# Block-diagonal copies on GpSimd, transposes of 104 partitions, loads of 48 rows and new offsets in the list

## The chip, the cores and the metric

The kernel runs on one core of one Trainium2 chip. The metric is the device time of one execution in microseconds (us). TensorE is called PE in the profile (its weight loads PEld), VectorE DVE, ScalarE ACT, GpSimd POOL, and SyncE, which issues part of the DMAs, SP.

## The reference

Two parts, one after the other. The first is a recurrence with a 40 x 40 state for each of 4 batches and 8 heads over 768 steps:

```python
for t in range(S):
    y[:, :, t] = np.einsum('bhd,bhde->bhe', rt, state)
    Sa = np.einsum('bhde,bhe->bhd', state, at)
    state_decay = state * wt[:, :, None, :] - np.einsum('bhd,bhe->bhde', Sa, bt)
    state = state_decay + np.einsum('bhd,bhe->bhde', vt, kt)
```

The second is an MLP on the 3072 tokens of width 320 that come out of it: `h = x @ w_in` with 2048 columns, `g = h * tanh(softplus(h))`, and `g @ w_out` back to 320. All is float32.

## The kernel before

**Tiling.** The 768 steps are cut into 12 chunks of 64. The 32 heads (batch and head together) are split by two bits, be and al, and by 8 places s. Of a tile's 128 partitions, al chooses the lower or the upper 64, and 40 of each 64 hold the head's 40 dimensions: partitions 0 to 39 and 64 to 103 are used, the rest is zero or filler. The first 104 partitions so hold all that is used.

**Preparation of a chunk, `pre_a(c, be)`** (24 calls). SP loads w and a (tile wa, L322) and b and k (tile bk, L325), each in two DMAs of 40 rows, one for al=0 and one for al=1. VectorE forms running products of w by two scans (L343, L348), scales a in place (L346) and b, k (L354). ScalarE copies a into the block-diagonal tile ad (L352), two copies of 64 partitions. TensorE multiplies ad by bk in groups of 3, 3 and 2 places (L386); the results go to GP and HA (L389 to L397). TensorE then transposes bk by a matmul with the identity in cst, four at a time into one PSUM bank (L410), and ScalarE copies the 40 used columns of each 64 to bkn (L412). GpSimd's queue writes P out to pD (L357).

**Inversion, `inv(n)`** (6 calls, one for each two chunks). VectorE transposes GP into X (L420), runs 30 steps of two small instructions each (L425, L428) that invert all 32 x 32 triangles of the two chunks at once, and transposes the result to TT (L430) and T1 (L432). TensorE forms the lower-left blocks of the 64 x 64 inverses (L444, L452) with a copy by ScalarE between them (L454). For each chunk and be ScalarE then fills the block-diagonal tile bdT: the two diagonal blocks from TT for each al (L466, L467) and the off-diagonal one from PSUM (L468). TensorE multiplies it with HA (L476), ScalarE evicts to KT (L479).

**Steps, `step(c)`** (12 calls). For each half g of the places: `step_a` copies the state ST into VS (L504), multiplies with KT (L514) and evicts u to UVT (L517); `step_b` multiplies UVT by r's block-diagonal tile bdr (L557) and masks into UVQ (L560); `step_u` transposes UVT (L528, L530); `step_d` transposes the state (L544) and evicts it to smd (L546); `step_c` multiplies UVQ by bkn (L586) and smd by bdr (L591), adds the state (L596, L602) and copies y out (L598). The state passes from chunk to chunk, so the steps of a chunk wait for those of the one before. `step_loads` fills VS, UVT and bdr for the next chunk by GpSimd's queue (L487, L491, L494); each of these tiles has one buffer, so the load waits for the last reader of the chunk before.

**MLP.** `convert` loads w_in and w_out and splits them into a high and a low part on ScalarE and VectorE (tile cv, L731 to L739). `load_x` reads y and P back and multiplies them (L792 to L797). `mlp1` (L814) and `mlp2` (L835 to L837) run 6 x 8 times.

**The order.** The program is written as a list of operations, each with the engine, a booked duration, what it reads and writes and, for a DMA, its latency (`lat`) and service time (`srv`). `Plan.order` simulates the engines with these booked numbers and at each point takes, among the ready operations of the engine that is free first, the one with the highest priority: the length of the work that hangs behind it plus an offset from PRIO, by the operation's kind and its chunk (kinds such as 'ld' the loads of a chunk, 'pv' its VectorE part, 'ik' bdT and KT, 'wi' the conversion of w_in). Operations that become ready within LOOK plus an entry of LOOKS of the earliest may be chosen as well. The order that comes out is fixed: each engine and each DMA queue then runs its instructions strictly in it.

The planner books ScalarE's copy to ad like this:

```python
        for al in range(2):
            q = slice(al * 64, al * 64 + 64)
            op('A', 0.62, lambda q=q, al=al: A.copy(ad[q, :, :, al], a[q].rearrange("p (s k t) -> p s k t", k=2, t=32)),
               r=[('a', be, al)], w=[('ad', be, al)])
```

## Time and profile before

| | |
|---|---|
| time, median of 3 runs | 746.27 us (744.09 to 746.48) |
| the profiled execution | 745.79 us, of it 744.0 us span |
| mean granted TensorE clock | 0.965 |
| instructions | 17243 |
| busy, share of the span | PE 91%, PEld 84%, DVE 61%, ACT 57%, POOL 14% |
| DMA | 58206 packets, 61.81 MB |

The span runs from the first to the last instruction of the profiled execution. "Busy" is the time in which an engine worked on at least one instruction; a matmul's end is modelled, and matmuls overlap, so the mean duration of a matmul is longer than the pace at which they follow each other. A line such as "L410 PE MATMUL ps<-cst,bk 128*128 128x128 f32 x192 | 25.4, 282 | 2.4" gives the line in the kernel, the engine and operation, what is written from what (moving operand, then stationary), the shapes (stationary 128*128, moving 128x128), the count, busy us, mean ns of one, and the idle time ahead of them with what ended it. A piece of the chain of waits has its start, its length and what it was. A wait row gives the engine and line that waited, for whom, us in total, how often, and the longest.

### The profile page before, as it was taken

How to read it: one execution, taken by the hardware profiler on the slowest of the kernel's cores; microseconds unless marked ns; L12 is line 12 of the kernel's file. 1: busy time of each engine (PE TensorE's matmuls, PEld its weight loads, DVE VectorE, ACT ScalarE, POOL GpSimd, SP SyncE). 2: the span in 40 equal slices, each digit the busy share in tenths (PEclk: the TensorE clock that was granted, in tenths of full speed). 3: DMA queues.
4: the chain of work that ended last, by engine and by line, in shares of the span. 5: the costliest groups of instructions: out<-in, count | busy, mean ns of one | idle time of the engine just before them, and what ended most of it. 6: DMA issues, size and time to landing. Idle time of an engine off the chain costs nothing.

```text
span 744.0 us, 17243 instructions
## 1 busy us (share of the span) xinstructions
...
## 2 busy tenths in 40 slices
...
GB/s 191 171 98 89 64 39 104 77 139 116 107 109 111 101 118 150 37 117 128 123 220 185 206 46 100 0 12 97 14 1 103 18 1 40 19 0 1 36 1 35
DMA packets 58206, 61.81 MB, mean 83 GB/s; under 512 B 25536, under 2 KB 48704, under 8 KB 58128
## 3 DMA queue, kind: packets, MB, share of 16 engines
...
## 4 chain that ended last, share of the span: by engine, by line
PE 64%; DVE 22%; ACT 7%; issue 4%; DMA 1%; POOL 0%; ACTq 0%; DVEq 0%
PE ps L814 24%; PE ps L835 7%; PE ps L837 7%; PE ps L836 7%; PE ps L557 4%; DVE XL L428 3%; DVE tmp L425 3%; PE ps L386 3%; PE ps L586 3%; DVE P L343 2%; DVE bk L354 2%; PE ps L476 2%; PE ps L528 2%; DVE HA L394 2%; PE ps L591 1%
## 5 line engine op out<-in xcount | busy, mean ns | idle before, releaser
L819 DVE TENSOR_TENSOR gl<-g,gh 128x1024 fp32r<-128x1024 f32 x48 | 58.8, 1225 | 194.9 <-ACT gh L818 188.7
L817 ACT ACTIVATE g<-ps 128x512 f32<-128x512 f32 x96 | 57.0, 597 | 173.6 <-PE ps L814 173.3
L837 PE MATMUL ps<-w_oh,gl 128*128 128x320 f32 x384 | 118.6, 309 | 0.0
L835 PE MATMUL ps<-w_oh,gh 128*128 128x320 f32 x384 | 118.5, 309 | 0.0
L836 PE MATMUL ps<-w_ol,gh 128*128 128x320 f32 x384 | 118.5, 309 | 0.0
L814 PE MATMUL ps<-xh,w_ih 128*128 128x512 f32 x288 | 113.2, 393 | 0.0
L814 PE MATMUL ps<-xh,w_il 128*128 128x512 f32 x288 | 97.7, 393 | 0.0
L386 PE MATMUL ps<-bk,ad 128*128 128x168 f32 x384 | 68.7, 340 | 26.9 <-DVE bk L354 18.2
L386 PEld LDWEIGHTS ps<-bk,ad 128*128 128x128 f32 x384 | 63.8, 215 | 28.8 <-issue 26.5
L814 PE MATMUL ps<-xl,w_ih 128*128 128x512 f32 x192 | 75.4, 393 | 0.0
L836 PEld LDWEIGHTS ps<-w_ol,gh 128*128 128x128 f32 x384 | 72.1, 188 | 2.1
L835 PEld LDWEIGHTS ps<-w_oh,gh 128*128 128x128 f32 x384 | 72.1, 188 | 2.0
L837 PEld LDWEIGHTS ps<-w_oh,gl 128*128 128x128 f32 x384 | 72.1, 188 | 0.0
L814 PEld LDWEIGHTS ps<-xh,w_il 128*128 128x128 f32 x288 | 54.1, 188 | 12.3
L814 PEld LDWEIGHTS ps<-xh,w_ih 128*128 128x128 f32 x288 | 54.2, 188 | 10.6 <-issue 0.2
L428 DVE TENSOR_TENSOR XL<-XL,tmp 128x30 f32<-128x30 f32 (+9 forms) x180 | 58.7, 326 | 2.0
L425 DVE TENSOR_TENSOR tmp<-XL 128x30 f32<-128x30 f32 (+9 forms) x180 | 58.5, 325 | 1.7
L557 PE MATMUL ps<-bdr,UVT 128*128 128x128 f32 x384 | 48.8, 283 | 4.9 <-ACT UVT L517 2.7
L818 ACT CAST gh<-g 128x1024 fp32r<-128x1024 f32 x48 | 50.4, 1050 | 1.5
L557 PEld LDWEIGHTS ps<-bdr,UVT 128*128 128x128 f32 x384 | 46.1, 197 | 6.0 <-ACT UVT L517 3.4
L476 PE MATMUL ps<-bdT,HA 128*104 128x128 f32 x384 | 46.9, 280 | 2.4 <-ACT bdT L468 2.4
L476 PEld LDWEIGHTS ps<-bdT,HA 128*104 128x104 f32 x384 | 44.1, 174 | 4.1 <-ACT bdT L468 2.2
...
## 6 DMA issues: line engine op xcount, KB each, us to landing
...
```

The costliest lines, as they stand in the source:

```text
L386: PE.matmul(pv()[:, j], ad[:, s0 + j].rearrange("p k a t -> p (k a t)"), bk[:, s0 + j], start=(j == 0), stop=True, skip_group_check=True)
L425: op('V', (0.16 + m * i * 0.00104), lambda tv=tv, i=i, m=m: V.tensor_tensor(out=tv, in0=X[:, i + 1:32, i:i + 1].broadcast_to([128, m, i]), ...
L428: op('V', (0.16 + m * i * 0.00104), lambda tv=tv, i=i: V.tensor_tensor(out=X[:, i + 1:32, 0:i], in0=X[:, i + 1:32, 0:i], in1=tv, op=ALU.ad ...
L476: PE.matmul(kv()[:, j], ha.t[:, s0 + j], bd[:, o + s0 + j].rearrange("p a t -> p (a t)"), start=(j == 0), stop=True, skip_group_check=True)
L557: PE.matmul(qv()[:, s], UVT[:, g * 4 + s, be * 128:be * 128 + 128], bdr[:, be, g * 4 + s].rearrange("p a t -> p (a t)"), start=(s == 0), s ...
L814: PE.matmul(b.t, w, x, start=(n == 0), stop=(n == 7), skip_group_check=True)
L817: op('A', 0.6, lambda b=b, j=j: A.activation(g.t[:, j], b.t, AF.Mish), r=[b], w=[(g, j)])
L818: op('A', 1.05, lambda: A.copy(gh.t, g.t), r=[(g, 0), (g, 1)], w=[gh])
L819: op('V', 1.226, lambda: V.tensor_tensor(out=gl.t, in0=g.t, in1=gh.t.bitcast(F32), op=ALU.subtract), r=[(g, 0), (g, 1), gh], w=[gl])
L835: PE.matmul(o, gh.t[:, j, t], oh, start=(f == 0 and j == 0), stop=False, skip_group_check=True)
L836: PE.matmul(o, gh.t[:, j, t], ol, start=False, stop=False, skip_group_check=True)
L837: PE.matmul(o, gl.t[:, j, t], oh, start=False, stop=(f == 7 and j == 1), skip_group_check=True)
```

## The change

- The copies of a into ad (L352) and of the diagonal blocks from TT into bdT (L466, L467) go from ScalarE to GpSimd, booked at 0.6 and 0.35 us.
- The transposes of bk, UVT and the state (L410, L528, L544) read partitions 0 to 103 and use a 104 x 104 identity; four results of 104 columns lie side by side in the bank, and the evictions pick the two times 40 used columns out of each (`heads`). smd keeps 320 elements and 24 of filler, set to zero once, in place of 512.
- The host arrays for w and a, b and k, r and v are padded from 40 to 48 rows per half, and the DMAs move 48 rows. Their booked service times fall.
- PRIO has new numbers in all its rows, and LOOKS, empty before, has entries.

The diff, with the two lists cut to a few rows:

```diff
 LOOK = 0.05
-LOOKS = {}
+LOOKS = {
+    'zero': (0.05, 0.05, 0.15, 0.05, 0.1, 0.1, 0.05,),
+    'ld': (1, 0.05, 0.05, 0,),
...
+}
 PRIO = {
...
-    'wi': (-64.5, -663.5, 78, 201.5, 248.5, 158.5, 616, 742, 588, 148, 305, 685.5,),
...
+    'wi': (-1016, -754.5, -442, -504.5, -596.5, -768, -478, -268.5, -156, -212.5, -71.5, -34.5,),
...
 }
...
     r, k, vv, w, a, b = (v(inp[n]) for n in 'rkvwab')
     o = {}
     wt = w.transpose(4, 2, 1, 6, 3, 0, 5).reshape(nch, 2, 2, 40, 8, C)
-    wa = np.zeros(wt.shape[:4] + (1040,), np.float32)
-    wa[..., :520].reshape(wt.shape[:4] + (8, 65))[..., 1:] = wt
-    wa[..., 528:] = a.transpose(4, 2, 1, 6, 3, 0, 5).reshape(nch, 2, 2, 40, 512)
+    wa = np.zeros((nch, 2, 2, 48, 1040), np.float32)
+    wa[..., 40:, :520].reshape(nch, 2, 2, 8, 8, 65)[..., 1:] = 1
+    wa[..., :40, :520].reshape(nch, 2, 2, 40, 8, 65)[..., 1:] = wt
+    wa[..., :40, 528:] = a.transpose(4, 2, 1, 6, 3, 0, 5).reshape(nch, 2, 2, 40, 512)
     o['wa'] = wa
     bt, kt = (x.transpose(4, 2, 1, 6, 3, 0, 5).reshape(nch, 2, 2, 40, 8, 1, C) for x in (b, k))
     bk = np.concatenate([bt, kt], -2)
     bk[:, 1] = np.concatenate([kt, bt], -2)[:, 1]
-    o['bk'] = bk.reshape(nch, 2, 2, 40, 8, 128)
-    o['rD'] = np.ascontiguousarray(r.transpose(4, 1, 6, 2, 3, 0, 5)).reshape(nch, 2, 40, 16, C)
-    o['vD'] = np.ascontiguousarray(vv.transpose(4, 1, 6, 3, 0, 2, 5)).reshape(nch, 2, 40, 8, 128)
+    pad = lambda x, ax: np.concatenate([x, np.zeros(x.shape[:ax] + (8,) + x.shape[ax + 1:], np.float32)], ax)
+    o['bk'] = pad(bk.reshape(nch, 2, 2, 40, 8, 128), 3)
+    o['rD'] = pad(r.transpose(4, 1, 6, 2, 3, 0, 5).reshape(nch, 2, 40, 16, C), 2)
+    o['vD'] = pad(vv.transpose(4, 1, 6, 3, 0, 2, 5).reshape(nch, 2, 40, 8, 128), 2)
     o['vN'] = np.ascontiguousarray(vv.transpose(4, 2, 5, 3, 0, 1, 6)).reshape(nch, 2, C, 16, 40)
     p = np.arange(128)
     cst = np.zeros((128, 328), np.float32)
...
 
     cst = cs.tile([128, 328], F32, name="cst")
     ident = cst[:, 0:128]
+    used = slice(0, 104)
+    rows = cst[used, 0:104]
+    heads = lambda x: bass.AP(x.tensor, x.offset, [x.ap[0], [104, 4], [64, 2], [1, 40]])
     maskQ = cst[:, 128:192]
     maskH = cst[:, 192:256]
     maskG = cst[:, 296:328]
...
     newRW = make(wk, 4, [128, 2, 16], "rw")
     newR = make(wk, 2, [128, 2, 4], "R")
     newSTN = make(wk, 2, [128, 8, 40], "stn")
-    newSMD = make(wk, 2, [128, 4, 128], "smd")
+    newSMD = make(wk, 2, [128, 344], "smd")
     newYEV = make(wk, 1, [128, 2, 8, 64], "yev")
     newHA = make(ci, NHA, [128, 8, 104], "HA")
     newGP = make(ci, 2, [128, 32, 2, 32], "GP")
...
         op('G', 0.7, lambda t=VS[be]: G.memset(t, 0.0), w=[(k, be, g) for k in ('VSv', 'VSs') for g in range(2)])
         op('G', 0.5, lambda t=ST[be]: G.memset(t, 0.0), w=[('ST', be)])
     op('G', 0.8, lambda: [G.memset(t[:, 640:664], 0.0) for t in S.bkn], w=['bkn0'])
+    op('G', 0.2, lambda: [G.memset(t[:, 320:344], 0.0) for t in S.smd], w=['smd0'])
 
     view = lambda b, p, n, pat, **k: b.t[p, 0:n].rearrange(pat, **k)
     full = slice(0, 128)
...
         wa, bk, ad = wab[be], bkb[be], adb[be]
         xo, og, ok, oa, oh = (0, 0, 64, 0, 40) if be == 0 else (0, 64, 0, 64, 0)
         for al in range(2):
-            q = slice(al * 64, al * 64 + 40)
-            op('S', 0.45, lambda q=q, al=al: SP.dma_start(out=wa[q], in_=I['wa'][c, be, al]), w=[('wz', be, al), ('a', be, al)], lat=1.95, srv=1.0)
+            q = slice(al * 64, al * 64 + 48)
+            op('S', 0.45, lambda q=q, al=al: SP.dma_start(out=wa[q], in_=I['wa'][c, be, al]), w=[('wz', be, al), ('a', be, al)], lat=1.95, srv=0.76)
         for al in range(2):
-            q = slice(al * 64, al * 64 + 40)
-            op('S', 0.82, lambda q=q, al=al: SP.dma_start(out=bk[q, :, xo:xo + 128], in_=I['bk'][c, be, al]), w=[('bk', be, al)], lat=2.65, srv=1.08)
+            q = slice(al * 64, al * 64 + 48)
+            op('S', 0.82, lambda q=q, al=al: SP.dma_start(out=bk[q, :, xo:xo + 128], in_=I['bk'][c, be, al]), w=[('bk', be, al)], lat=2.65, srv=0.82)
         if (c, be) == (0, 0):
             op('S', 0.4, lambda: SP.dma_start(out=cst, in_=I['cst']), w=['cst'], lat=1.8, srv=0.95)
             for b, t, o in zip(range(2), bkb, (128, 128)):
...
                                                    initial=0.0, op0=ALU.mult, op1=ALU.add), r=WZ + ['d1'], w=['E'])
         for al in range(2):
             q = slice(al * 64, al * 64 + 64)
-            op('A', 0.62, lambda q=q, al=al: A.copy(ad[q, :, :, al], a[q].rearrange("p (s k t) -> p s k t", k=2, t=32)),
+            op('G', 0.6, lambda q=q, al=al: G.tensor_copy(ad[q, :, :, al], a[q].rearrange("p (s k t) -> p s k t", k=2, t=32)),
                r=[('a', be, al)], w=[('ad', be, al)])
         op('V', 1.22, lambda: V.tensor_tensor(out=bk4, in0=bk4, in1=E3[:, :, 0:64].unsqueeze(2).broadcast_to([128, 8, 2, 64]),
                                               op=ALU.mult), r=['E'], w=BK)
...
         bkn = BKN[c, be] = newBKN()
         for s0 in (0, 4):
             b = newPS()
-            pv = lambda b=b: view(b, full, 512, "p (s a e) -> p s a e", s=4, a=2)
+            pv = lambda b=b: view(b, full, 416, "p (s x) -> p s x", s=4)
 
             def tr(s0=s0, pv=pv):
                 for j in range(4):
-                    PE.transpose(pv()[:, j].rearrange("p a b -> p (a b)"), bk[:, s0 + j, xo:xo + 128], ident)
-            op('P', 0.44, tr, r=BK + ['cst', 'bkn0'], w=[b], mode=128, work=0.42, claim=[bkn])
-            op('A', 0.43, lambda s0=s0, pv=pv: A.copy(bkn.t[:, s0 * 80:s0 * 80 + 320].rearrange("p (s a e) -> p s a e", a=2, e=40),
-                                                     pv()[:, :, :, 0:40]), r=[b], w=[(bkn, s0)])
+                    PE.transpose(pv()[:, j], bk[used, s0 + j, xo:xo + 128], rows)
+            op('P', 0.357, tr, r=BK + ['cst', 'bkn0'], w=[b], mode=128, work=0.347, claim=[bkn])
+            op('A', 0.43, lambda s0=s0, b=b: A.copy(bkn.t[:, s0 * 80:s0 * 80 + 320].rearrange("p (s a e) -> p s a e", a=2, e=40),
+                                                   heads(b.t)), r=[b], w=[(bkn, s0)])
 
     def inv(n):
         S.at('iv', 2 * n)
...
                 for al in range(2):
                     q0 = slice(al * 32, al * 32 + 32)
                     q1 = slice(64 + al * 32, 96 + al * 32)
-                    op('A', 0.4, lambda bd=bd, q0=q0, us=us, al=al: A.copy(bd[q0, :, al, 0:32], TT[q0, us]), r=['TT'], w=[bdk[al * 3]])
-                    op('A', 0.4, lambda bd=bd, q1=q1, us=us, al=al: A.copy(bd[q1, :, al, 32:64], TT[q1, us]), r=['TT'], w=[bdk[al * 3 + 1]])
+                    op('G', 0.35, lambda bd=bd, q0=q0, us=us, al=al: G.tensor_copy(bd[q0, :, al, 0:32], TT[q0, us]), r=['TT'], w=[bdk[al * 3]])
+                    op('G', 0.35, lambda bd=bd, q1=q1, us=us, al=al: G.tensor_copy(bd[q1, :, al, 32:64], TT[q1, us]), r=['TT'], w=[bdk[al * 3 + 1]])
                     op('A', 0.37, lambda bd=bd, q0=q0, al=al, yv=yv, be=be: A.copy(bd[q0, :, al, 32:64], yv()[q0, be * 8:be * 8 + 8]), r=[by],
                        w=[bdk[al * 3 + 2]])
                 for s0 in (0, 4):
...
             op('G', 0.65, lambda be=be: G.dma_start(out=VS[be][vrow[be], :, 0:320], in_=I['vN'][c, be].rearrange("i (g s) d -> i g (s d)", g=2)),
                w=[('VSv', be, 0), ('VSv', be, 1)], lat=2.3, srv=0.7)
         for al in range(2):
-            q = slice(al * 64, al * 64 + 40)
-            op('G', 0.75, lambda q=q, al=al: G.dma_start(out=UVT[q, :, 64:192], in_=I['vD'][c, al]), w=[('UVv', al, 0), ('UVv', al, 1)], lat=2.9, srv=0.85)
+            q = slice(al * 64, al * 64 + 48)
+            op('G', 0.75, lambda q=q, al=al: G.dma_start(out=UVT[q, :, 64:192], in_=I['vD'][c, al]), w=[('UVv', al, 0), ('UVv', al, 1)], lat=2.9, srv=0.65)
         for al in range(2):
-            q = slice(al * 64, al * 64 + 40)
+            q = slice(al * 64, al * 64 + 48)
             op('G', 0.85, lambda q=q, al=al: G.dma_start(out=bdr[q, :, :, al].rearrange("p b s t -> p (b s) t"), in_=I['rD'][c, al]),
-               w=[('bdr', al, 0), ('bdr', al, 1)], lat=3.3, srv=1.1)
+               w=[('bdr', al, 0), ('bdr', al, 1)], lat=3.3, srv=0.85)
 
     UV = lambda g: [('UVv', 0, g), ('UVv', 1, g), ('u', g)]
 
...
         if c < nch - 1:
             for be in range(2):
                 b = newPS()
-                tv = lambda b=b: view(b, full, 512, "p (s a d) -> p s a d", s=4, a=2)
+                tv = lambda b=b: view(b, full, 416, "p (s x) -> p s x", s=4)
 
                 def tr(be=be, tv=tv):
                     for s in range(4):
-                        PE.transpose(tv()[:, s].rearrange("p a d -> p (a d)"), UVT[:, g * 4 + s, be * 128:be * 128 + 128], ident)
-                op('P', 0.44, tr, r=UV(g) + ['cst'], w=[b], mode=128, work=0.42)
-                op('A', 0.43, lambda be=be, tv=tv: A.copy(UVQ[be][:, g * 8:g * 8 + 8, 64:104], tv()[:, :, :, 0:40].rearrange("p s a d -> p (s a) d")),
+                        PE.transpose(tv()[:, s], UVT[used, g * 4 + s, be * 128:be * 128 + 128], rows)
+                op('P', 0.357, tr, r=UV(g) + ['cst'], w=[b], mode=128, work=0.347)
+                op('A', 0.43, lambda be=be, b=b: A.copy(UVQ[be][:, g * 8:g * 8 + 8, 64:104].rearrange("p (s a) d -> p s a d", a=2), heads(b.t)),
                    r=[b], w=[('U', be, g)])
 
     def step_d(c, g):
...
         if c == 0:
             return None
         smd, b = newSMD(), newPS()
-        dv = lambda: view(b, full, 512, "p (s x) -> p s x", s=4)
+        dv = lambda: view(b, full, 416, "p (s x) -> p s x", s=4)
 
         def tr():
             for s in range(4):
-                PE.transpose(dv()[:, s], st[:, 2 * s:2 * s + 2].rearrange("p a d -> p (a d)"), ident)
-        op('P', 0.44, tr, r=[('ST', g), 'cst'], w=[b], mode=128, work=0.42)
-        op('A', 0.58, lambda: A.copy(smd.t, dv()), r=[b], w=[smd])
+                PE.transpose(dv()[:, s], st[used, 2 * s:2 * s + 2].rearrange("p a d -> p (a d)"), rows)
+        op('P', 0.357, tr, r=[('ST', g), 'cst'], w=[b], mode=128, work=0.347)
+        op('A', 0.43, lambda: A.copy(smd.t[:, 0:320].rearrange("p (s a d) -> p s a d", a=2, d=40), heads(b.t)), r=[b, 'smd0'], w=[smd])
         return smd
 
     def step_b(c, g):
...
                 if c > 0:
                     for j in range(2):
                         for be in range(2):
-                            PE.matmul(py[be * 64:be * 64 + 64, 2 * j:2 * j + 2, 0:64], smd.t[:, s0 + j, be * 64:be * 64 + 64],
+                            PE.matmul(py[be * 64:be * 64 + 64, 2 * j:2 * j + 2, 0:64], smd.t[:, (s0 + j) * 80 + be * 40:(s0 + j) * 80 + be * 40 + 64],
                                       bdr[:, be, g * 4 + s0 + j], start=False, stop=True, skip_group_check=True)
             op('P', 1.15 if c else 0.72, mm, r=[(k, h) for k in bkns for h in (0, 4)] + [(x, be, g) for x in 'QU' for be in range(2)] +
                ([smd] if smd else []) + [('bdr', 0, g), ('bdr', 1, g)], w=[b], lat=0.2, mode=64, work=1.1 if c else 0.69)
...
 
     def convert(self, hl, src, after, key):
         nc, S = self.tc.nc, self.S
-        V, A, SP, op = nc.vector, nc.scalar, nc.sync, S.op
+        V, A, SP, G, op = nc.vector, nc.scalar, nc.sync, nc.gpsimd, S.op
         n = src.shape[1]
         x = n / 1000
         H, L = (lambda: hl()[0]), (lambda: hl()[1])
```

2 lines of the change are left out of this document (1 added, 1 removed), and 76 rows, old and new, of tables (LOOKS, PRIO).

## The prediction

> **What bounds the kernel now.** I read the busy time by stretch first. In the row, after the stretch and its length, come busy us (and instructions) of PE, PEld, DVE, ACT and POOL, then the granted TensorE clock, the DMA share and GB/s.
>
> ```profile
> 0.00:12.00 12.00, 0.00 (x0) 0.00 (x0) 7.48 (x15) 6.46 (x10) 11.47 (x22) 1.00 0.64 182
> 12.00:108.00 96.00, 58.74 (x597) 55.33 (x598) 93.24 (x220) 52.27 (x153) 15.94 (x31) 0.75 0.37 104
> 108.00:345.00 237.00, 229.01 (x3685) 215.52 (x3685) 224.63 (x578) 188.95 (x501) 64.03 (x98) 1.00 0.42 109
> 345.00:394.00 49.00, 44.78 (x851) 42.24 (x851) 29.23 (x56) 36.71 (x81) 9.78 (x14) 0.97 0.58 147
> 394.00:744.00 350.00, 346.09 (x1920) 312.91 (x1919) 101.44 (x111) 136.43 (x196) 1.01 (x2) 1.00 0.17 47
> ```
>
> There are four different kernels in this span. Up to 108 us VectorE sets the pace (93.24 of 96 busy) while TensorE is 39% idle. From 108 to 345 both are full: TensorE 229.0 of 237, VectorE 224.6. From 345, after the sixth inversion, VectorE is free (29 of 49) and the last two chunks run as a chain through TensorE and ScalarE. From 394 the MLP keeps TensorE busy without a gap; the change touches nothing there, so 350 us are fixed and all that can move is the time at which the MLP starts.
>
> The chain that ended last says the same: MLP matmuls apart, it changes hands between the engines.
>
> ```profile
> PE 64%; DVE 22%; ACT 7%; issue 4%; DMA 1%; POOL 0%; ACTq 0%; DVEq 0%
> 256.32 4.16 DMA bdr<-in_rD
> 380.13 4.46 DMA bdr<-in_rD
> 342.68 2.01 DVE L430 STREAM_TRANSPOSE TT<-XL 128x1024 f32<-128x1024 f32 x1
> ```
>
> 22% of 744 is 164 us of VectorE, 7% is 52 us of ScalarE, nearly all ahead of 394, and POOL is not on it: the engine that receives work carries none of the chain today. The two DMA pieces are TensorE's chain standing still for r; the last row is the end of the sixth inversion, at 344.7.
>
> **The change, part by part.** The profiled execution took 745.79 us (span 744.0, 1.8 around it), 0.5 below the median of 746.27. I sum against 745.79.
>
> (1) *Transposes of 104.* The moving operand (cst, the identity) shrinks from 128 to 104 columns.
>
> ```profile
> L410 PE MATMUL ps<-cst,bk 128*128 128x128 f32 x192 | 25.4, 282 | 2.4 <-ACT ad L352 2.4
> L528 PE MATMUL ps<-cst,UVT 128*128 128x128 f32 x176 | 22.8, 275 | 1.0 <-ACT UVT L517 1.0
> L544 PE MATMUL ps<-cst,ST 128*128 128x128 f32 x88 | 13.6, 279 | 1.1 <-DVE ST L602 1.1
> 208.45 0.87 PE ps L410 x8
> 190.91 4.56 PE ps L386 x32
> 321.53 2.02 PE ps L514 x64
> ```
>
> The means of 275 to 282 ns overlap, so I take the pace from the chain: 0.87/8 = 109 ns for 128 columns, 0.85 ns each; L386 with 168 columns gives 4.56/32 = 142.5 ns, 0.85 again, so columns set the pace. 24 fewer save 20.4 ns, and 192+176+88 = 456 transposes save 9.3 us of TensorE. Below it is bounded by 0: if loading 128 weight columns set the 109 ns, nothing would change. L514 speaks against that: pairs that load 2 x 64 columns take 2 x 2.02/64 = 63 ns. Of the 9.3 us, the part before 108 lies under VectorE, and in 108 to 345 VectorE has only 12.4 us of idle time to let TensorE run ahead into. I take **-6** (0 to -9.3).
>
> (2) *Copies from ScalarE to GpSimd.*
>
> ```profile
> L352 ACT COPY ad<-wa 64x512 f32<-64x512 f32 x48 | 29.6, 617 | 13.3 <-issue 6.8 <-DVE wa L346 4.6 <-ACT bkn L412 0.9
> L466 ACT COPY bdT<-TT 32x256 f32<-32x256 f32 x48 | 19.4, 403 | 2.0 <-PE ps L476 0.7 <-DVE TT L430 0.5
> L467 ACT COPY bdT<-TT 32x256 f32<-32x256 f32 x48 | 19.2, 401 | 0.9
> L546 ACT COPY smd<-ps 128x512 f32<-128x512 f32 x22 | 12.9, 589 | 0.4 <-PE ps L544 0.2
> L842 ACT COPY os<-ps 128x320 f32<-128x320 f32 x24 | 9.7, 426 | 20.0 <-DMA out<-os 13.3 <-PE ps L837 6.7
> ```
>
> ScalarE loses 29.6+19.4+19.2 = 68.2 us, and 22 x (589-426) = 3.6 us more because smd is now evicted as 320 elements, the shape of the L842 row: 72 of the 278 us it works in 12 to 394. TensorE's idle time from 108 to 394 is 8.0+4.2 = 12.2 us, and that is the most this can return there. The copies that stand on the chain itself are those after the sixth inversion, 16 in a row, 6.4 us of ScalarE beside KT's evictions; GpSimd does them beside ScalarE. I take **-4** (0 to -12).
>
> What they cost on GpSimd no row shows, since no GpSimd instruction in this trace reads SBUF. Nearest are its fills:
>
> ```profile
> L303 POOL MEMSET bdT<- 128x1024 f32 x2 | 1.8, 951 | 0.0
> POOL VS L487 <- PE ps L514: 53.8, 9, 12.4
> POOL UVT L491 <- PE ps L557: 53.0, 7, 12.9
> SPq L322 <- ACT ad L352: 30.6, 12, 12.7
> ```
>
> 0.93 ns an element makes 0.48 and 0.24 us; reading as well could double that. The diff books 0.6 and 0.35, inside these bounds and near ScalarE's 0.62 and 0.40; I take those: 48 x 0.6 + 96 x 0.35 = 62 us, which beside the POOL column's 101 in 394 us fits. But POOL's queue is in order, and in it v, u and r loads wait for TensorE up to 12.9 us at a time. A copy behind such a load is late, then the L386 group that needs ad, and on SP's queue the next wa load (L322), which waits for ad's copy. The list decides that order, so I price it with (5).
>
> (3) *The list.* Its "wi" offsets fall (first four: -64.5, -663.5, 78, 201.5 become -1016, -754.5, -442, -504.5), so w_in's conversion goes later.
>
> ```profile
> 0.00:108.00 108.00, 7.71 (x12) 0.78 0.40 112
> 345.00:394.00 49.00, 13.73 (x23) 0.97 0.58 147
> ```
>
> These are VectorE's instructions on cv alone. 7.7 us lie in the part where VectorE is the bound; after 345 it has 19.8 us free, so they would be hidden there. But the MLP cannot start without the first quarter of w_in. I take **-4** (0 to -7.7). Everything else the list reorders I can't price and leave to the range.
>
> (4) *Loads of 48 rows.* 8 more rows of 40, so 20% more bytes for wa, bk, v and r.
>
> ```profile
> DMA to landing us min/median/max: 3.7/4.5/6.0
> ```
>
> This is bdr's. Between the shortest landing (0.8 less) and 20% more (0.9 more), on the two pieces of the chain: -1.6 to +1.8. The Trainium skill, "DMA: Bandwidth & Descriptors", section "Why a DMA increments its semaphore by 16 and not by 1", says that a transfer goes over the largest number of engines up to 16 that divides its outer dimension: 10 for 40 rows, 16 for 48, so 3 rows an engine instead of 4; no row here shows the split, and by it the term would be -2.2, estimated as a quarter of 4.5 twice. I take **-1**.
>
> (5) *GpSimd beside VectorE.* What a copy that reads SBUF does to VectorE this trace can't show. VectorE's instructions with both inputs in SBUF are mostly these:
>
> ```profile
> L428 DVE TENSOR_TENSOR XL<-XL,tmp 128x30 f32<-128x30 f32 (+9 forms) x180 | 58.7, 326 | 2.0
> L425 DVE TENSOR_TENSOR tmp<-XL 128x30 f32<-128x30 f32 (+9 forms) x180 | 58.5, 325 | 1.7
> L343 DVE TENSOR_TENSOR_SCAN P<-wa,d 128x520 f32<-128x520 f32 x24 | 29.6, 1233 | 0.1
> L348 DVE TENSOR_TENSOR_SCAN E<-wa,d 128x519 f32<-128x519 f32 x24 | 29.5, 1230 | 0.1
> L354 DVE TENSOR_TENSOR bk<-bk,E 128x1024 f32<-128x1024 f32 x24 | 29.0, 1209 | 0.1
> L346 DVE TENSOR_TENSOR wa<-wa,P 128x512 f32<-128x512 f32 x24 | 16.4, 684 | 0.0
> 9.01 1.24 DVE L343 TENSOR_TENSOR_SCAN P<-wa,d 128x520 f32<-128x520 f32 x1
> 8.98 1.95 POOL L494 DMA_DIRECT2D bdr<-in_rD  x2
> ```
>
> Together 221.7 us of the 317.9 that VectorE works between 12 and 345, 70%. Up to 344.7 about 47 x 0.6 + 80 x 0.35 = 56 us of copies run (the last inversion's 16 come after). From nothing to 0.7 x 56 = 39 us of stall, then. The last two rows are the nearest: a scan beside a GpSimd instruction, at 1.24 us the usual length, nothing lost; but that one does not read SBUF. VectorE's idle time in 12 to 345 is 333-317.9 = 15 us and takes that much of a stall. I take 18 us, under half of 39: **+3** (0 to +24).
>
> Sum: -6 -4 -4 -1 +3 = -12, so 745.8-12 = **734 us**.
>
> **Rivals.** *The engine lock (slower).* Each GpSimd copy holds up the VectorE instruction behind it, and VectorE, already the bound, becomes slower: it runs through the scans right after L346, where ad's copies fall, and the 360 steps of the inversions. Then TensorE waits anyway and (1) is worth nothing: 745.8 -4 -4 -1 + (s-15), slower than before from a stall s of 24 us, 61% of 39. Midway between 24 and 39 it gives some **753**; with all 39, 761. For it: VectorE's 95% busy and 70% share. Against: no stall beside the POOL instructions seen so far, and 16 copies that fall where VectorE is free. The Trainium skill, "SBUF — State Buffer", section "Who interferes with whom", says just this: a VectorE instruction with two SBUF inputs and a GpSimd instruction that reads SBUF exclude each other for the whole instruction, and speaks against this change; no run here shows it yet.
>
> *VectorE stays the bound (same).* TensorE's and ScalarE's savings are hidden under VectorE, the sixth inversion still ends near 345, what the conversions free goes into stalls, and only the tail gives 1 or 2 us: **745**. For it: 93 of 96 and 225 of 237 busy, and nothing in the diff shortens a VectorE instruction. Against: the idle 12 us of TensorE and 15 of VectorE.
>
> *The transposes don't shrink.* Weight loads keep 109 ns: the sum without (1), **740**. L514's 63 ns speaks against it.
>
> **How the numbers follow.** Forecast 0.52 (721 to 743), shorter than that 0.05, transposes unchanged 0.08, same 0.11, lock 0.24. About 0.3%, 2.2 us, is what a measurement of this kernel can tell from no change. Faster 0.65, same 0.11, slower 0.24. The range runs from 721 (all of (1), half of (2)'s bound, (3) full, without a stall: 745.8-9.3-6-7.7-1.6 = 721) to 754, which leaves out the 0.05 below and the upper half of the lock rival.
>
> **What would show it.** Right: the first long L814 stretch starts near 382 instead of 393.8; 8 transposes on the chain take 0.71 us instead of 0.87; ScalarE's busy time falls by some 70 us; L343, L348, L354 and L425 keep their means of 1233, 1230, 1209 and 325 ns; the cv conversions move behind 108; bdr lands under 4.5 us. Wrong: those means grow, or gaps open ahead of them released by POOL (the lock); L386 or SP's L322 waits for POOL copies that stood behind a load (the queue's order); or the sixth inversion still ends at 345.

## The result and the profile after

| | before | after |
|---|---|---|
| time, median | 746.38 us (744.09 to 747.80, 4 runs) | 775.73 us (774.83 to 776.02, 4 runs) |
| ratio, 95% interval | | 1.0394 [1.0374, 1.0414] |
| span of the profiled execution | 744.0 us | 773.8 us |
| mean granted clock | 0.965 | 0.935 |

Ratios, here and below, are taken from the runs that lie within 1.5% of their kernel's fastest.

The changed kernel is 29.4 us slower. The forecast was 734.0, and 754 the end of its range. The lines of the changed functions stand 33 further down: the scan L343 is now L376, ad's copy L352 is L385, the inversion's L425 and L428 are L458 and L461, TT's transpose L430 is L463, the first MLP product L814 is L847.

The page of after: the span, the busy row and the chain that ended last.

```profile
span 773.8 us, 17277 instructions
...
PE 687.5 (89%) x7048; PEld 633.7 (82%) x7048; DVE 471.4 (61%) x975; ACT 349.0 (45%) x793; POOL 189.9 (25%) x312
...
PE 62%; DVE 21%; DMA 6%; issue 5%; ACT 2%; POOL 2%; SPq 0%; DVEq 0%; ACTq 0%; POOLq 0%
```

ScalarE gave up 71.8 us, as forecast, and its share of the chain fell from 7% to 2%. That freed nothing: DMA has gone from 1% to 6% and POOL from 0 to 2%, and VectorE, which was given no new work, is busy 15.4 us longer. The stretches of after, with the same columns as in the prediction:

```profile
12.00:108.00 96.00, 51.14 (x468) 48.16 (x470) 92.34 (x204) 30.29 (x109) 40.35 (x60) 0.70 0.54 120
108.00:378.00 270.00, 249.35 (x3863) 234.15 (x3861) 243.02 (x598) 149.68 (x424) 122.22 (x198) 0.93 0.47 109
378.00:424.00 46.00, 41.18 (x812) 38.68 (x809) 27.68 (x51) 28.65 (x62) 15.02 (x29) 0.96 0.66 156
424.00:774.00 350.00, 345.85 (x1919) 312.71 (x1918) 101.31 (x113) 136.16 (x196) 1.00 (x2) 1.00 0.18 48
```

The MLP takes its 350 us as before. It starts near 424 in place of 394, because the sixth inversion ends near 378 in place of 345: all of the loss is ahead of that point, and the tail behind it is even shorter (46 us against 49). In the long stretch TensorE is granted 0.93 of its clock, where it had 1.00.

VectorE's instructions with both inputs in SBUF, and GpSimd's copies, by line (busy us, mean ns, idle time ahead of them):

```profile
L461 DVE TENSOR_TENSOR XL<-XL,tmp 128x30 f32<-128x30 f32 (+9 forms) x180 | 63.5, 353 | 1.7
L458 DVE TENSOR_TENSOR tmp<-XL 128x30 f32<-128x30 f32 (+9 forms) x180 | 62.1, 345 | 1.6
...
L381 DVE TENSOR_TENSOR_SCAN E<-wa,d 128x519 f32<-128x519 f32 x24 | 31.0, 1290 | 0.2
L387 DVE TENSOR_TENSOR bk<-bk,E 128x1024 f32<-128x1024 f32 x24 | 31.0, 1290 | 1.1 <-DMA bk<-in_bk 0.9
...
L385 POOL COPY ad<-wa 64x512 f32<-64x512 f32 x48 | 41.3, 861 | 27.8 <-issue 15.9 <-DVE wa L379 4.4 <-ACT bkn L445 2.0
L500 POOL COPY bdT<-TT 32x256 f32<-32x256 f32 x48 | 27.4, 570 | 2.6
L499 POOL COPY bdT<-TT 32x256 f32<-32x256 f32 x48 | 26.2, 545 | 13.2 <-PE ps L509 6.1 <-DVE TT L463 4.2 <-DVE d L375 0.8
```

Every mean that the prediction named as a sign of the lock has grown (L343 from 1233 to 1258 ns, L348 from 1230 to 1290, L354 from 1209 to 1290, L425 from 325 to 345). The copies take 94.9 us, not the 62 that the diff's bookings give. The timeline shows single cases; columns are start, length, engine and line:

```profile
12.70 1.64 DVE L376 TENSOR_TENSOR_SCAN P<-wa,d 128x520 f32<-128x520 f32 x1
...
16.07 1.64 DVE L381 TENSOR_TENSOR_SCAN E<-wa,d 128x519 f32<-128x519 f32 x1
...
198.08 1.24 DVE L376 TENSOR_TENSOR_SCAN P<-wa,d 128x520 f32<-128x520 f32 x1
...
198.24 1.27 POOL L499 COPY bdT<-TT 32x256 f32<-32x256 f32 x1
```

In the first two a scan is 0.41 us longer than its usual 1.23: copies to ad ran from 11.09 to 13.24 and from 15.26 to 16.62. In the last pair it is the other way round: the scan keeps its 1.24 us, and a copy that takes 0.39 us at its shortest lasts until 0.19 us after the scan's end. In these cases whoever came second waited. Most copies don't meet such an instruction: of L499's 48 the median takes 392 ns, the longest 1343.

### The profile page after: what moved, and what is told of

Its sections match the earlier page's. It is cut to its first block, busy times and chain, and to the rows that moved or that the text cites. A ratio compares the mean times of both kernels' runs of the same rounds, so it can differ in the third digit from the quotient of the medians.

```text
span 773.8 us, 17277 instructions
## 1 busy us (share of the span) xinstructions
PE 687.5 (89%) x7048; PEld 633.7 (82%) x7048; DVE 471.4 (61%) x975; ACT 349.0 (45%) x793; POOL 189.9 (25%) x312
## 4 chain that ended last, share of the span: by engine, by line
PE 62%; DVE 21%; DMA 6%; issue 5%; ACT 2%; POOL 2%; SPq 0%; DVEq 0%; ACTq 0%; POOLq 0%
PE ps L847 23%; PE ps L870 7%; PE ps L868 7%; PE ps L869 7%; DVE XL L461 4%; DVE tmp L458 4%; PE ps L590 4%; DMA cv<-in_wi 3%; PE ps L619 3%; PE ps L419 2%; PE ps L547 2%; DVE HA L427 2%; PE ps L624 1%; DVE bk L387 1%; DMA bdr<-in_rD 1%
## 5 line engine op out<-in xcount | busy, mean ns | idle before, releaser
L847 PE MATMUL ps<-xh,w_ih 128*128 128x512 f32 x288 | 113.2, 393 | 0.0
L847 PE MATMUL ps<-xh,w_il 128*128 128x512 f32 x288 | 97.7, 393 | 0.0
L847 PE MATMUL ps<-xl,w_ih 128*128 128x512 f32 x192 | 75.4, 393 | 0.0
L461 DVE TENSOR_TENSOR XL<-XL,tmp 128x30 f32<-128x30 f32 (+9 forms) x180 | 63.5, 353 | 1.7
L847 PEld LDWEIGHTS ps<-xh,w_il 128*128 128x128 f32 x288 | 54.1, 188 | 12.3
L458 DVE TENSOR_TENSOR tmp<-XL 128x30 f32<-128x30 f32 (+9 forms) x180 | 62.1, 345 | 1.6
L847 PEld LDWEIGHTS ps<-xh,w_ih 128*128 128x128 f32 x288 | 54.2, 188 | 10.6 <-ACT yev L631 0.2
L509 PE MATMUL ps<-bdT,HA 128*104 128x128 f32 x384 | 49.9, 291 | 1.3 <-ACT bdT L501 1.0
L509 PEld LDWEIGHTS ps<-bdT,HA 128*104 128x104 f32 x384 | 47.2, 184 | 2.4 <-POOL bdT L500 1.3
```

The source lines that it names most:

```text
L458: op('V', (0.16 + m * i * 0.00104), lambda tv=tv, i=i, m=m: V.tensor_tensor(out=tv, in0=X[:, i + 1:32, i:i + 1].broadcast_to([128, m, i]), ...
L461: op('V', (0.16 + m * i * 0.00104), lambda tv=tv, i=i: V.tensor_tensor(out=X[:, i + 1:32, 0:i], in0=X[:, i + 1:32, 0:i], in1=tv, op=ALU.ad ...
L509: PE.matmul(kv()[:, j], ha.t[:, s0 + j], bd[:, o + s0 + j].rearrange("p a t -> p (a t)"), start=(j == 0), stop=True, skip_group_check=True)
L847: PE.matmul(b.t, w, x, start=(n == 0), stop=(n == 7), skip_group_check=True)
```

## The experiments

"Old order" below is before's list with before's booked numbers. Only the engine that executes an operation, or its operands, are exchanged, so the operations keep the sequence that was planned. Each ratio is to the kernel before on the same chip. The median of the kernel before lay between 746.4 and 749.0 us on the chips used, so a difference of times from different chips is uncertain by 2 or 3 us, and the ratios are the safer comparison. The diffs show only the call inside an operation; its engine and its booked times in the list stay.

**The parts alone, in the old order.** First the copies (e4):

```diff
-A.copy(ad[q, :, :, al], a[q].rearrange("p (s k t) -> p s k t", k=2, t=32))
+G.tensor_copy(ad[q, :, :, al], a[q].rearrange("p (s k t) -> p s k t", k=2, t=32))
...
-A.copy(bd[q0, :, al, 0:32], TT[q0, us])
+G.tensor_copy(bd[q0, :, al, 0:32], TT[q0, us])
...
-A.copy(bd[q1, :, al, 32:64], TT[q1, us])
+G.tensor_copy(bd[q1, :, al, 32:64], TT[q1, us])
```

> The kernel of before with its order kept, only the 144 copies done by GpSimd in place of ScalarE. The one part that the lock needs, without the new loads, transposes and list. Lock expects a loss of 10 to 35 us, 756 to 781, with the inversion's instructions at 340 to 355 ns on average and copies that wait up to 1 us and more. Loads and list expect 735 to 750, since ScalarE is relieved and nothing else is changed.

764.83 us, ratio 1.0248 [1.0224, 1.0272]: this part alone costs 18.4 us. The groups by line:

```profile
L425 DVE TENSOR_TENSOR tmp<-XL 128x30 f32<-128x30 f32 (+9 forms) x180 | 64.7, 360 | 1.8
L428 DVE TENSOR_TENSOR XL<-XL,tmp 128x30 f32<-128x30 f32 (+9 forms) x180 | 63.6, 353 | 2.0
...
L352 POOL COPY ad<-wa 64x512 f32<-64x512 f32 x48 | 40.3, 840 | 19.0 <-issue 13.5 <-DVE wa L346 2.5 <-PE ps L386 0.8
```

The stretch from 12 us to the end of the sixth inversion, in before and in e4, with the columns of the prediction:

```profile
12.00:344.70 332.70, 287.45 (x4277) 270.55 (x4278) 317.57 (x797) 240.92 (x652) 79.98 (x129) 0.93 0.41 108
```
```profile
12.00:362.60 350.60, 293.61 (x4277) 275.86 (x4278) 333.15 (x796) 181.24 (x525) 166.64 (x258) 0.92 0.38 102
```

The stretch is 17.9 us longer. VectorE is busy 15.6 us longer in it (333.15 less 317.57), and it idles 17.5 us where it idled 15.1: its idle time took nothing of the stall.

To part what a read costs from what the place in GpSimd's queue costs, two kernels fill ad and bdT on GpSimd instead of copying; both leave out the copying of a and of the inverses. The first (e8) still copies one element ahead of each fill:

```diff
-G.tensor_copy(ad[q, :, :, al], a[q].rearrange("p (s k t) -> p s k t", k=2, t=32))
+(G.tensor_copy(ad[q, 0:1, 0, al, 0:1], a[q, 0:1].unsqueeze(1)), G.memset(ad[q, :, :, al], 0.0))
...
-G.tensor_copy(bd[q0, :, al, 0:32], TT[q0, us])
+(G.tensor_copy(bd[q0, 0:1, al, 0:1], TT[q0, us][:, 0:1, 0:1]), G.memset(bd[q0, :, al, 0:32], 0.0))
```

> The same replacement in the kernel of before with its order, whose copies moved to GpSimd cost 18 us. It leaves out the copying of a and of the inverses: ad and bdT hold zeros. Lock expects the 18 us gone and something of ScalarE's relief to show: 738 to 749. If GpSimd's queue or its dispatch make the 18 us, it stays at 758 to 768.

758.03 us, 1.0144 [1.0126, 1.0163]: at the lower edge of what was expected if GpSimd's queue or dispatch made the loss, and far from the 738 to 749 of the lock. The same stretch, then groups by line:

```profile
12.00:357.40 345.40, 292.12 (x4278) 274.26 (x4279) 318.68 (x797) 181.43 (x525) 178.28 (x386) 0.93 0.40 104
...
L428 DVE TENSOR_TENSOR XL<-XL,tmp 128x30 f32<-128x30 f32 (+9 forms) x180 | 58.8, 327 | 2.0
...
L352 POOL MEMSET ad<- 64x512 f32 x48 | 25.0, 521 | 13.5 <-PE ps L386 10.8
...
L467 POOL COPY bdT<-TT 32x1 f32<-32x1 f32 x48 | 20.5, 428 | 2.1
```

The second (e10) reads nothing at all. Its fills of bdT no longer wait for TT either, and they have no small instruction ahead of them:

```diff
-(G.tensor_copy(ad[q, 0:1, 0, al, 0:1], a[q, 0:1].unsqueeze(1)), G.memset(ad[q, :, :, al], 0.0))
+(G.memset(a[q, 0:1], 0.0), G.memset(ad[q, :, :, al], 0.0))
...
-(G.tensor_copy(bd[q0, 0:1, al, 0:1], TT[q0, us][:, 0:1, 0:1]), G.memset(bd[q0, :, al, 0:32], 0.0))
+G.memset(bd[q0, :, al, 0:32], 0.0)
```

> The same in the kernel of before with its order: fills only on GpSimd in place of the 144 copies of ScalarE. It leaves out the copying of a and of the inverses. If the 11 us that were left with one-element copies come from their waits for VectorE, they go and ScalarE's relief shows: 735 to 747. If they come from the places of the copies in GpSimd's queue, behind loads that wait, it stays at 752 to 760.

745.68 us, 0.9981 [0.9964, 0.9998], with 68 us of copies gone from ScalarE.

The three in a row: VectorE's durations are back as soon as the reads are short (e8: busy 318.68 us, L428 at 327 ns). So it is the reads that lengthen VectorE's instructions, and in e4 VectorE's longer work is 15.6 of the 17.9 us.

What e8 still loses is of another kind. VectorE idles 26.7 us there (345.40 less 318.68), 15.5 in e10, and only 17.5 in e4. A copy of one element to bdT lasts 428 ns in the mean (L467; the other two lines 325 and 319), and GpSimd has 144 instructions more than in e4. From e8 to e10 another 12.4 us go, but three things change at once: no read, 96 instructions fewer, and no wait for TT, for which GpSimd stood 7.4 us in e8. No run parts these three, so the 12.4 us can't be put down to copies that wait for VectorE. For ad, whose fills still wait for a, the place in GpSimd's queue costs nothing that shows in e10; for bdT that is not shown. The net gain of e10 over before is 1.4 us by the ratio (0.1 to 2.7): ScalarE's relief brings little.

Next the transposes (e5), with the change's own edits of L410, L528, L544, smd and `heads` and nothing else of it:

```diff
-PE.transpose(pv()[:, j].rearrange("p a b -> p (a b)"), bk[:, s0 + j, xo:xo + 128], ident)
+PE.transpose(pv()[:, j], bk[used, s0 + j, xo:xo + 128], rows)
```

> The kernel of before with its order kept and only the transposes of 104 partitions with their evictions (smd as 320 elements). If columns set the pace and TensorE is on the path, 456 times 20 ns show in part: 738 to 744, and 8 transposes take 0.71 us. If weight loads set the pace, 8 take 0.87 us and nothing moves: 745 to 748. If TensorE's saving is hidden under VectorE, 8 take 0.71 us and the time stays at 744 to 747.

The transposes of 104 with the shorter smd: 746.44 us, 0.9984 [0.9966, 1.0002], no difference that can be told from none. TensorE does get faster (before: 282, 275, 279 ns), and 8 transposes on the chain take down to 0.71 us (0.87 before):

```profile
L413 PE MATMUL ps<-cst,bk 104*128 104x104 f32 x192 | 21.3, 261 | 2.4 <-ACT ad L355 2.4
...
L547 PE MATMUL ps<-cst,ST 104*128 104x104 f32 x88 | 11.9, 259 | 1.6 <-DVE ST L605 1.5
```

The sixth inversion's end moves from 344.7 to 342.9, as VectorE sets it, and the MLP starts at 389.7 in the profiled execution, which was the fastest of the twelve (741.79 us); of 4 us there about 1 shows in the medians.

Then the loads (e6), with the change's own padding on the host and its 48 rows in the four DMAs:

```diff
-q = slice(al * 64, al * 64 + 40)
+q = slice(al * 64, al * 64 + 48)
```

> The kernel of before with its order kept and only the loads of 48 rows. If a transfer of 48 rows goes over more DMA engines, bdr lands in 3.6 us instead of 4.5 and the time falls by 1 to 3 us: 743 to 746. If only the bytes count, it lands later and the time is 746 to 750.

Loads of 48 rows alone: 751.42 us, 1.0063 [1.0047, 1.0078], some 4 us slower. The first 12 us by engine:

```profile
0.00:12.00 12.00, 0.00 (x0) 0.00 (x0) 8.16 (x14) 6.05 (x9) 11.46 (x23) 1.00 0.94 175
```

And bdr's landing, from the view of that tile:

```profile
DMA to landing us min/median/max: 3.7/4.5/7.9
```

In these 12 us the DMA engines are busy for 0.94 instead of 0.64, and move 175 GB/s instead of 182. The share fits more engines taking part in each transfer, though no row counts them. They bring no more bytes a second, and there are 20% more bytes in the padded loads. The landing's median stays at 4.5 us, and its maximum goes from 6.0 to 7.9.

**The whole change without its list.**

The edits of e5, e6 and e10 in one kernel (e13):

> The order and the booked costs of before, with every other part of the change: transposes of 104 partitions, loads of 48 rows, and the 144 copies taken off ScalarE, as GpSimd fills that read no SBUF (which leaves out copying a and the inverses). From the single parts: the fills 745.7, the transposes -1, the loads +4, so 747 to 751 if the parts add up. The kernel after without reads took 763.6, so the new order's own price would then be 13 to 16 us. If 760 or more, the parts hurt each other, and the order is not to blame.

All parts but the list, with fills that read nothing: 746.84 us, 0.9996 [0.9974, 1.0018]. The 4 us of the loads do not show here.

The edits of e4, e5 and e6 in one kernel (e14):

> The whole change but its list and its booked costs: the order of before, with the copies on GpSimd, transposes of 104 partitions and loads of 48 rows. Parts that add up give 764.8 - 1 + 4 = 768. Against 775.7 the new list would have cost about 8 us on top. If the new list is what makes the loss, under 760; if the list did the other parts good, 776 or more.

The same with the real copies: 764.19 us, 1.0220 [1.0189, 1.0251]. From 746.8 to 764.2, 17.4 us, is copies in place of fills: by the traces VectorE is busy 14.3 us longer up to the end of the sixth inversion (333.12 us against 318.79), so most of it is GpSimd's reads, and bdT's wait for TT is at most in the rest. The list then adds another 11.5 us, to 775.7.

**The new order.** The kernel after, with one thing taken back each time. Its copies on ScalarE again (e1):

```diff
-G.tensor_copy(ad[q, :, :, al], a[q].rearrange("p (s k t) -> p s k t", k=2, t=32))
+A.copy(ad[q, :, :, al], a[q].rearrange("p (s k t) -> p s k t", k=2, t=32))
...
-G.tensor_copy(bd[q0, :, al, 0:32], TT[q0, us])
+A.copy(bd[q0, :, al, 0:32], TT[q0, us])
```

> The changed kernel with its order of instructions kept, but the 144 copies to ad and bdT done by ScalarE again. Three theories stand. Lock: a GpSimd copy and a VectorE instruction with two SBUF inputs exclude each other; VectorE's stalls and the late copies make the loss of 29 us. Loads: the 48-row loads move 4.7 MB more and land later. List: the new order is worse whatever engine does the copies. Lock expects most of the loss gone, 745 to 755 us, with L458 and L461 back at a mean of 325 ns from 345 and 353. Loads expects 770 or more. List expects 768 or more.

792.67 us (784.50 to 795.14), 1.0583 [1.0518, 1.0649]. ScalarE now has to run the 144 copies at places planned for another engine, so this kernel is worse than after, and the comparison doesn't part the lock from the order; the runs with fills do. Loads of 40 rows of the padded arrays (e2), for w and a, b and k, r and v:

```diff
-q = slice(al * 64, al * 64 + 48)
+q = slice(al * 64, al * 64 + 40)
...
-in_=I['wa'][c, be, al]
+in_=I['wa'][c, be, al, 0:40]
```

> The changed kernel with its order kept, but with loads of 40 rows for w and a, b and k, v and r, as before. Lock expects no change beyond 3 us: 773 to 779. Loads expects most of the 29 us back: 750 or less, with the median landing of bdr back from 5.0 to 4.5 us. List expects 773 to 779.

777.35 us, 1.0404 [1.0361, 1.0448]: nothing won. The old list on after's operations and bookings (e3), that is PRIO of before and

```diff
-LOOKS = {
-    'zero': (0.05, 0.05, 0.15, 0.05, 0.1, 0.1, 0.05,),
...
-}
+LOOKS = {}
```

> The changed kernel with the list of before (its PRIO, and no LOOKS). The order changes everywhere, since the booked times of the changed operations stay. Lock expects no gain over the changed kernel, 765 to 785, with L458 and L461 still at 340 to 355 ns. Loads expects the same. List expects 755 or less.

793.31 us, 1.0631 [1.0603, 1.0660]. The old offsets are no better where they were not fitted: with other bookings, the same PRIO gives another order. "The old order" has to be tried with the old bookings, as in the runs above.

And after with the edits of e8 (e7), then with those of e10 (e9):

> The changed kernel with its order kept; each of the 144 GpSimd copies is replaced by a copy of one element (which keeps the wait for a or TT) and a fill of the same shape, so that GpSimd writes as much but no longer reads SBUF along with VectorE. It leaves out the copying of a and of the inverses: ad and bdT hold zeros. Lock (GpSimd's reads exclude VectorE's two-input instructions) expects that most of the 29 us comes back: 735 to 752, L458 and L461 at a mean of 325 ns. If instead the order, the loads or the move to GpSimd's queue make the loss, it stays at 765 or more. Between the two, 752 to 765, the lock is one part and the order another.

766.85 us, 1.0242 [1.0196, 1.0289]; VectorE's means are back at 325 and 326 ns. That is above both bands that gave the lock a part, though 8.9 us less than after.

> The changed kernel with its order kept; the 144 GpSimd copies become fills only, with no read of SBUF at all (ad's fill waits for the scaled a by a one-element fill into the tile that L379 wrote; bdT's fill does not wait for TT). It leaves out the copying of a and of the inverses. GpSimd then neither holds VectorE up nor waits for it, and its instructions take about what the planner booked. If the exclusion, by stall and by lateness together, makes the loss, 735 to 752. If the new order is bad in itself, or the loads of 48 rows are, it stays at 757 or more.

763.59 us, 1.0213 [1.0182, 1.0244]. So in the new order the reads cost 12.1 us (775.7 to 763.6), and 17 us over the kernel before are left in which GpSimd reads nothing. Against e13, which has the same parts in the old order, these 16.8 us are the order's own (16.2 by the ratios). The step from one-element copies to none, 12.4 us in the old order, is 3.3 us here (e7 to e9), and the two intervals overlap. So what copies cost by coming late is not a fixed price.

The stretch from 12 us to the end of the sixth inversion in e13 and in e9:

```profile
12.00:345.70 333.70, 279.80 (x4280) 263.89 (x4281) 318.79 (x802) 176.68 (x525) 128.46 (x311) 0.93 0.55 120
```
```profile
12.00:367.90 355.90, 296.81 (x4330) 280.25 (x4332) 320.36 (x802) 179.96 (x531) 127.28 (x303) 0.88 0.51 114
```

VectorE has 1.6 us more to do in the new order, but it idles 35.5 us instead of 14.9, without any read of GpSimd's.

Where the 16.8 us go shows in the starts of TT's transpose, which ends each inversion (us, from the timelines):

| | 1st | 2nd | 3rd | 4th | 5th | 6th |
|---|---|---|---|---|---|---|
| before | 86.0 | 127.5 | 183.5 | 241.8 | 301.7 | 342.7 |
| e13, old order, no reads | 87.7 | 129.0 | 186.4 | 244.2 | 303.2 | 343.7 |
| e9, new order, no reads | 89.8 | 129.1 | 186.2 | 260.6 | 322.5 | 365.9 |
| after | 93.0 | 134.5 | 192.9 | 270.5 | 334.0 | 376.3 |

Up to the third inversion the two orders are level (186.4 and 186.2). From there to the fourth the old takes 57.8 us, the new 74.4, and after 77.6. Of these 16.6 us some 7 are VectorE work that the new order has moved there (it is busy 61.99 us in e9, 55.02 in e13); in the rest it idles. Followed into that stretch, the chain of after shows the place (start, length, what):

```profile
198.19 0.13 PE ps L590
198.32 3.64 issue
201.96 1.41 PE ps L590 x7
203.37 1.85 PE ps L485 x64
205.22 2.00 PE ps L590 x8
```

TensorE starts one output product, stands still for 3.64 us with no releaser, and is then at half pace: 8 of these matmuls take 2.00 us, against 0.87 for 8 of the same width at the full clock (the transposes in the prediction). Two stretches of after, with the columns as above, the granted clock third from the end:

```profile
198.00:203.00 5.00, 1.36 (x11) 1.17 (x8) 1.29 (x2) 0.70 (x2) 4.77 (x9) 0.95 0.50 124
203.00:213.00 10.00, 10.00 (x184) 9.42 (x185) 6.08 (x9) 2.30 (x6) 3.34 (x5) 0.51 0.42 107
```

One idle gap, and the clock is 0.51 for the next 10 us. The Trainium skill, "TensorE: Matmul & The Clock Gate", section "HAM oscillation — how this bites in real kernels", warns of idle gaps over about 3.4 us, after which the clock is at half; this row agrees. Shorter gaps do not keep to it. Two more, the first pair from after, the second from e5 (the gap stands in brackets, then the stretch behind it):

```profile
232.34 0.55 PE L577 MATMUL ps<-cst,ST 104*128 104x104 f32 x4 [1.59 <-DVE ST L635]
...
233.00:240.00 7.00, 7.00 (x87) 6.10 (x85) 5.28 (x14) 3.48 (x10) 0.47 (x1) 0.51 0.90 186
```
```profile
382.23 2.02 PE L560 MATMUL ps<-bdr,UVT 128*128 128x128 f32 x16 [2.56 <-DMA bdr<-in_rD]
...
383.00:390.00 7.00, 7.00 (x125) 6.71 (x124) 6.34 (x11) 3.34 (x7) 0.00 (x0) 1.00 0.74 225
```

A gap of 1.59 us has half the clock behind it, one of 2.56 us the full clock. In this the measurement differs from the Trainium skill: the length of one gap does not decide. Over all the work between 100 us and the MLP (the four kernels in the order before, e13, e9, after):

```profile
100.00:394.00 294.00, 281.55 (x4674) 265.15 (x4674) 261.51 (x654) 233.31 (x598) 74.83 (x114) 0.99 0.44 113
```
```profile
100.00:394.00 294.00, 275.60 (x4685) 260.14 (x4684) 263.07 (x661) 178.31 (x486) 111.32 (x258) 0.99 0.55 125
```
```profile
100.00:413.00 313.00, 290.63 (x4697) 274.02 (x4696) 264.81 (x660) 180.49 (x488) 111.64 (x258) 0.94 0.50 117
```
```profile
100.00:424.00 324.00, 297.53 (x4716) 279.59 (x4711) 278.70 (x669) 182.36 (x494) 140.41 (x233) 0.93 0.49 114
```

What is the stall? It lies inside one group of four matmuls, between the first and the second; the operation's waits stand ahead of the first, and the trace shows no releaser. The DMA queues of after, once from 188 to 203 us and once from 199 to 200 (packets, MB, share of 16 engines):

```profile
q8 instruction: 1, 0.02, 0.5%
...
q8 instruction: 1, 0.02, 8.2%
```

The instruction queue has one packet in these 15 us, and it falls inside the stall. The loads of b and k, r and w and the write of y run together ahead of it; in e9, where the stall is 3.93 us, the DMA share around it (191 to 196) is 1.06. Three kernels thin out these transfers. The first (e12) is e9 with the loads of e2:

> The kernel after with its order and without GpSimd's reads of SBUF (fills in place of the 144 copies, which leaves out copying a and the inverses), and with loads of 40 rows again. With 48 rows the same kernel took 763.6 us, some 17 us over the kernel before, although nothing excludes VectorE any more. If the larger loads make that rest, 745 to 753. If the new order itself does, since it was fitted to booked costs that the chip does not have, 758 to 764. In between, both have a share.

757.00 us (748.43 to 768.44), 1.0101 [1.0070, 1.0132]. The ratio stands on six of ten runs (748.43 to 757.04); by it 40 rows are worth some 8 us here, between the two bands, where they were worth nothing with the real copies (e2). The profiled execution (762.81) is not one of the six, so nothing is read from its trace. The second (e15) is e9 with r's load cut to one place of 16 from the second chunk on, the third (e17) has the loads of b and k cut to one place of 8 as well. e16 and e18 are the same cuts in e13:

```diff
-G.dma_start(out=bdr[q, :, :, al].rearrange("p b s t -> p (b s) t"), in_=I['rD'][c, al])
+G.dma_start(out=bdr[q, :, :, al].rearrange("p b s t -> p (b s) t"), in_=I['rD'][c, al]) if c == 0 else
+G.dma_start(out=bdr[q, 0, 0:1, al], in_=I['rD'][c, al, :, 0:1])
...
-SP.dma_start(out=bk[q, :, xo:xo + 128], in_=I['bk'][c, be, al])
+SP.dma_start(out=bk[q, :, xo:xo + 128], in_=I['bk'][c, be, al]) if c == 0 else
+SP.dma_start(out=bk[q, 0, xo:xo + 128], in_=I['bk'][c, be, al, :, 0])
```

> The kernel after with its order, GpSimd fills that read nothing in place of the copies (leaves out copying a and the inverses), and from the second chunk on the load of r cut to one of its 16 places (leaves out most of r). In the kernel with the whole load (763.6) TensorE stands still for 3.9 us in the output product that reads r, near 192 us, with no releaser shown, and the granted clock is then 0.51 for some 10 us. If that stall is r's load behind the other transfers, it goes, the clock stays near 1.00 there, the stretch between the third and the fourth inversion falls from 74 us to some 66, and the time to 753 to 758. If the stall is something else, it stays and the time stays at 760 to 764.

761.32 us, 1.0173 [1.0132, 1.0215]. The expectation for r as the cause was missed: the stall falls only from 3.93 to 2.72 us, and the clock still halves behind it, as the two stretches show:

```profile
190.00:194.00 4.00, 1.28 (x26) 1.16 (x20) 2.14 (x4) 1.33 (x3) 2.06 (x6) 1.00 1.07 175
194.00:204.00 10.00, 10.00 (x183) 9.53 (x184) 5.13 (x9) 2.30 (x6) 1.23 (x5) 0.55 0.29 76
```

> The control to the run before: the same cut of r's load in before's order, with fills, transposes of 104 and loads of 48 rows (leaves out the same). With the whole load this kernel took 746.8, its longest wait for r is below 3.4 us and its clock stays at 1.00 after 100 us. 742 to 747 if only what r's load does to the chain goes; if it falls as far as the kernel with the new order does, 740 or less, the cut load helps everywhere and says nothing of the new order.

742.81 us, 0.9926 [0.9904, 0.9948]: the control gains 4.0 us, the new order 2.3 (5.2 and 3.0 by the ratios).

> The run of the new order with the short load of r, and from the second chunk on the load of b and k cut to one of its 8 places as well (leaves out most of b and k). With r cut alone the stall near 191 us fell from 3.9 to 2.7 us and the clock still halved behind it; the stall stands between the first and the second matmul of one group of four, the DMA engines are at 0.99 then, and the one packet of the instruction queue lies in it. If TensorE waits there for its next instructions behind crowded DMA engines, the stall falls to 1.5 us or less, the clock stays at 1.00, the stretch from the third to the fourth inversion falls from 72 to 66 us or less, and the time from 761 to 751 to 757. If the crowding has nothing to do with it, the stall stays at 2.5 or more and the time at 758 or more.

749.59 us, 1.0034 [1.0008, 1.0061]. The chain at the same place:

```profile
188.28 0.13 PE ps L592
188.42 0.51 issue
188.92 0.94 PE ps L592 x7
...
190.99 1.09 PE ps L592 x8
```

The stall is 0.51 us, the 8 matmuls take 1.09, the clock is 1.00 from 190 to 200, and the third inversion is followed by the fourth after 65.1 us instead of 74.4, with VectorE idle for 3.2 of them instead of 12.4.

> The control in before's order: r's and b's and k's loads cut in the same way (leaves out the same). With r cut alone it took 742.8, with its longest late stall 1.6 us and the clock at 1.00. 739 to 743 if the smaller loads take only what is left of waits there. As far from the run of the new order as that one keeps above it is the price of the new order without its stall.

740.52 us, 0.9927 [0.9906, 0.9949].

So with the loads thinned out the new order gains 14.0 us (763.6 to 749.6) and the old one 6.3 (746.8 to 740.5). Of the 16.8 us between the orders, 7.7 go when the loads are cut, and 9.1 stay; by the ratios it is 8.2 and 8.0 of 16.2, and by the intervals both halves are uncertain by some 3 to 4 us (an estimate). The stall shrinks as the loads are thinned out, in one profiled execution of each kernel; whether the traffic does it or the new timing is not parted. That TensorE waits there for its next instructions is the reading that fits the place of the stall and of the packet; no run shows it by itself. What makes up the 9.1 us is open too. One candidate is the clock, which still falls in the new order and not in the old (e17 and e18, from 100 us to the MLP):

```profile
100.00:401.00 301.00, 284.12 (x4675) 268.14 (x4676) 260.80 (x649) 178.55 (x485) 105.67 (x257) 0.95 0.35 92
```
```profile
100.00:387.00 287.00, 271.86 (x4649) 256.58 (x4644) 260.54 (x656) 175.93 (x481) 105.71 (x257) 1.00 0.37 95
```

**What is worth keeping.** GpSimd's copies did no harm where VectorE is idle, behind the sixth inversion. This kernel (e11) is before with the transposes of 104, and with only the last 16 copies on GpSimd:

```diff
-A.copy(bd[q0, :, al, 0:32], TT[q0, us])
+(G.tensor_copy if n == nch // 2 - 1 else A.copy)(bd[q0, :, al, 0:32], TT[q0, us])
```

> The kernel of before with its order kept, with the transposes of 104 partitions and with only the 16 copies after the sixth inversion on GpSimd, where VectorE is free. If the exclusion costs only where VectorE works, this keeps the part of the idea that pays: 738 to 745, with TT at 341 as in the run with the transposes alone and the MLP 1 to 4 us earlier. If the copies come late behind the waiting loads in GpSimd's queue, 746 or more.

743.79 us, 0.9961 [0.9944, 0.9978], a little below before. The transposes alone gave 0.9984 [0.9966, 1.0002]; the intervals overlap, and from TT's start to the MLP the profiled executions take 49.9 us here and 48.9 in e5. So that these copies bring something is not shown, only that they do no harm. They take 390 and 450 ns in the mean:

```profile
L470 POOL COPY bdT<-TT 32x256 f32<-32x256 f32 x8 | 3.6, 450 | 0.5
L469 POOL COPY bdT<-TT 32x256 f32<-32x256 f32 x8 | 3.1, 390 | 5.1 <-DVE TT L433 3.1 <-PE ps L479 1.8
```

## Why the prediction was wrong

The account by medians: all parts without reads and without the list, +0.5 us; the copies' reads (with bdT's wait for TT), +17.4; the list, +11.5; together 29.4. The two prices depend on each other: with the list first it is 16.8 for the list and 12.1 for the copies.

- **(5) GpSimd beside VectorE** is the step that failed first. It took 18 us of stall, let VectorE's idle 15 us swallow most of it, and came to +3. The stall was sized well, though "under half of 39" was no more than a choice: in e4 VectorE is busy 15.6 us longer up to the end of the sixth inversion. What was wrong is that idle time takes it. VectorE idles 17.5 us there in e4, before 15.1, so the stall came out in full: the sixth inversion ends 17.9 us later. After does idle 30.6 us (366 less 92.34 and 243.02), but that is the order's: e9, in which GpSimd reads nothing, idles 35.5. Only there, where VectorE idles so much, does idle time take a part of the stall, some 5 of 15 us (after against e9). The rival named the right mechanism, and the Trainium skill's rule behind it was right: in "SBUF — State Buffer", section "Who interferes with whom", a GpSimd instruction that only writes does not contend. The trace agrees, with fills of 520 ns and VectorE at 326 and 325 ns in e10. The rival's price took off the same 15 us, and 9 us of gains: its 753 fell short of the 764 that this part gives by itself. Its chance of 0.24 rested in part on a scan beside a GpSimd instruction that reads nothing, which said nothing about a read.
- **(3) The list** was priced at -4 by the one thing that could be read from it, the conversions behind 108. These moved less than thought (VectorE's part of them ahead of 108 fell from 7.71 to 5.18 us), and the order as a whole costs 11.5 us, 16.8 where nothing reads. "Everything else the list reorders I can't price and leave to the range" was the failing sentence: the range had no such term above. In place of the -4 the runs show VectorE idle for 35.5 us instead of 14.9 and TensorE's clock at 0.94 instead of 0.99 (e9 and e13); about half of the price goes when the loads are thinned out, the rest is open. The diff's bookings could have warned. They gave the copies 0.6 and 0.35 us, measured are 0.86 and 0.56; they cut the loads' service by a quarter (1.0 to 0.76), and bdr's median landing is 5.0 us in after and 4.5 in before. That these bookings make the loss is not shown: e9's fills take 0.53 and 0.31 us, less than booked, and the order costs its 16.8 us there.
- **(4) Loads of 48 rows**: -1 was forecast, alone they cost +4 (e6), with the other parts in the old order nothing that shows (e13). The bounds, -1.6 to +1.8, looked at two landings on the chain and not at the engines' load. The Trainium skill's rule on 16 engines, which the prediction names, fits the share of 0.94 against 0.64, but the gain of 2.2 us estimated from it did not come: bdr's median landing stays at 4.5 us in e6.
- **(1) Transposes**: they shrink, as forecast, and the rival that they don't is out. But the 6 us were hidden under VectorE; about 1 us shows, and that is not clear of none. The rival *VectorE stays the bound* was right for this term.
- **(2) ScalarE**: 71.8 us were taken off as forecast. In the long stretch that gave next to nothing (e10). The tail is indeed 3.9 us shorter in after (from TT's start to the MLP 47.2 us against 51.1), which looks like the -4, but that is luck: in e4 and e14, with the same copies in the old order, it takes 50.7, and in e9, with no copy at all, 47.0. The new order made it shorter.
- **The signs** named in advance did their work: the means of L343, L348, L354 and L425 grew, and the MLP start moved to 424 in place of 382. A sign that was not named was the granted clock. It was 1.00 before from 108 to 345, and no term allowed that it could fall.
